# Reading the moving operand of the wide matmuls one column of each half in turn, in block attention followed by a feed-forward layer

## The chip, the cores and the metric

The kernel runs on one core of one Trainium2 chip. The metric is the device time of one execution in microseconds, lower is better; the figure of a kernel is the median of its runs.

## The reference

```python
scores = scale * np.matmul(q_c, k_c.transpose(0, 1, 2, 4, 3))   # chunks of 64 tokens, float32
attn = np.exp(scores - np.max(scores, axis=-1, keepdims=True))
attn = attn / (np.sum(attn, axis=-1, keepdims=True) + 1e-09)
out = np.matmul(attn, v_c)                                       # (8, 8, 576, 64)
x = out.transpose(0, 2, 1, 3).reshape(4608, 512)
h = x @ w_in                                                     # w_in (512, 2048), float64
g = h * np.cos(h)
return (g @ w_out).astype(np.float32)                            # w_out (2048, 512), float64
```

Attention works inside chunks of 64 tokens. Nearly all of the arithmetic is in the two products with `w_in` and `w_out`.

## The kernel before

The 4608 tokens are cut into 9 tiles of 512 (`TOK`). `w_in` and `w_out` are cut into 16 blocks each (`fc`, 128 of the 2048 inner features). A number that goes into a wide product is split into a high and a low part, both in the 4-byte type fp32r, and a product is made of three matmuls: high by high, high by low, low by high, all adding to the same bank of sums. So every product has three matmuls, each with a stationary operand of 128x128 (its weight load is an instruction of its own, PEld) and a moving operand of 128 partitions by 512 columns, or 256 in a few places.

- The hidden layer: `hidden` (line 859) for tiles 0 and 1, and `product` (line 1107) for the others, take a block of `w_in` (or sums and differences of blocks, "combos", kept in HBM and streamed back) as the stationary operand and the transposed tokens `x` as the moving one. The sums are `h` (in banks named h and a): 128 inner features on the partitions, 512 tokens as columns. Tile 2 (`FAST`) is paired with itself: two halves of 256 tokens, so its matmuls have 256 columns (`single_pair`). Tiles 3 to 8 go in pairs (`wide_pair`, `second_tile`), with 512 columns.
- `g = h cos h` is made by ScalarE and VectorE, split into `g_hi` and `g_lo` (lines 500 and 504; the low parts go to VectorE or GpSimd).
- The output layer: `projected_by_parts` (line 895) for tiles 0 and 1, and `out_part` (line 1160) for the others, take 128 columns of `g` (a quarter `sub` of the tile's tokens) as the stationary operand and a block of `w_out`, 512 columns, as the moving one. The sums are `acc`, one bank for each of four quarters: 128 tokens on the partitions, 512 output features as columns. They run over the blocks `fc`.
- `finish` (line 920) copies a bank of finished sums to SBUF (line 500 on ScalarE, line 498 on VectorE; for tile 0, whose first 8 blocks were stored apart as `partial`, line 939 adds) and stores 128 rows of the output (line 942), one DMA for each quarter. The last quarter of the last tile is made and stored in two halves of 256 output features.

All matmuls are issued by the one helper at line 494, so a row of the trace is told apart by its tiles: `h<-x,w_in`, `h<-w_in,w_in` and `a<-x,w_in` are hidden layer, `acc<-w_out,...` are output layer, `kt,qt` and `pts,vt` are attention. All DMAs are issued on SP's queue.

The order of the work is made when the program is built: each piece of work has an engine, a length, what it waits for, and a due time from long lists (`DUE_FIRST` and so on), and a planner (`placed`, `in_order`) lays them out; instructions then keep that order on each engine. The planner counts 0.68 us for three matmuls of 512 columns, 0.706 for six of 256 and 1.362 for six of 512.

```python
        matmul(o, g_hi[:, ss], w_hi[:, cols], start=first, stop=False, **on)
        matmul(o, g_hi[:, ss], w_lo[:, cols], start=False, stop=False, **on)
        matmul(o, g_lo[:, ss], w_hi[:, cols], start=False, stop=last, **on)
```

In `split_weight` (line 564, issued from the pieces it returns) ScalarE reads every second 4-byte word of the float64 weights, a read with a step of 8 bytes.

Of the kernel before, what the change touches and what calls it, by code (L numbers as in the profile page):

```python
# [21 lines left out]
P = 128  # L22
TOK = 512
# [12 lines left out]
FAST = 2  # L36
# [53 lines left out]
PE, ACT, DVE, POOL, SP = range(5)  # L90
# [369 lines left out]
def attention_then_cos_ffn(ctx: ExitStack, tc, qT, kT, v, w_in, w_out, out, wide):  # L460
# [4 lines left out]
    nc = tc.nc  # L465
    NT, HP = qT.shape[0], qT.shape[1]
    NFC, NCC = w_in.shape[1], w_in.shape[2]
    DM = out.shape[1]
    NCH = TOK // CH
    NSUB = TOK // P  # L470
# [15 lines left out]
    def kept(ins):  # L486
        tc.keep_in_program_order(ins)
        return ins
# [4 lines left out]
    def matmul(*args, **kw):  # L493
        kept(nc.tensor.matmul(*args, **kw))  # L494

    def copy_by(by, out, in_):
        if by == DVE:
            kept(nc.vector.tensor_copy(out, in_))
        else:
            kept(nc.scalar.copy(out=out, in_=in_))  # L500
# [13 lines left out]
    w_parts = {}  # L514
# [71 lines left out]
    x_parts = {}  # L586
# [9 lines left out]
    def x_room(t, dtype):  # L596

        kind = (t + (t > 1)) % 2
        asked_x[kind] += 1
        return x_named(f"x{kind}_{asked_x[kind] % 4}", dtype)  # L600
# [30 lines left out]
    def bank(kind, i):  # L631
        if kind == "a":
            b = ps_a.tile([P, 512], F32, name=f"a{i % 2}")
        else:
            b = ps_o.tile([P, 512], F32, name=f"acc{i}")
        return b
# [218 lines left out]
    acc = {}  # L855

    partial = [hbm.tile([P, DM], F32, name=f"partial{sub}") for sub in range(NSUB)]

    def hidden(t, fc, ccs=range(4), h=None):
        if h is None:  # L860
            h = ps_h.tile([P, TOK], F32, name="h")
        w_hi, w_lo = w_parts["in", fc]
        for cc in ccs:
            x_hi, x_lo = (x[:, cc % 2] for x in x_parts[t, cc // 2])
            ws = slice(cc * P, (cc + 1) * P)
            matmul(h, w_hi[:, ws], x_hi, start=(cc == 0), stop=False)
            matmul(h, w_hi[:, ws], x_lo, start=False, stop=False)
            matmul(h, w_lo[:, ws], x_hi, start=False, stop=(cc == NCC - 1))
        return h
# [25 lines left out]
    def projected_by_parts(s, sums_out):  # L895

        t, fc = order[s]
        first = s == 0 or order[s - 1][0] != t
        last = s == len(order) - 1 or order[s + 1][0] != t

        def part(sub):
            g_hi, g_lo = g_parts[t, fc]
            w_hi, w_lo = w_parts["out", fc]
            if first:
                acc[sub] = bank("acc", sub)
            o = acc[sub]
            ss = slice(sub * P, (sub + 1) * P)
            matmul(o, g_hi[:, ss], w_hi, start=first, stop=False)
            matmul(o, g_hi[:, ss], w_lo, start=False, stop=False)
            matmul(o, g_lo[:, ss], w_hi, start=False, stop=last)  # L910
            if last:
                sums_out.append(lambda by=None, sub=sub, o=o: finish(t, sub, o, fc == NFC - 1, by))

        return [lambda sub=sub: part(sub) for sub in range(NSUB)]

    def out_room(sub):

        return (wts if sub % 2 else dec).tile([P, DM], F32, name=f"half{sub // 2}" if sub % 2 else "w")

    def finish(t, sub, o, whole, by, cols=None):  # L920
        r0 = t * TOK + sub * P
        to = out[r0 : r0 + P, :]
        if t == 1 or not whole:

            os = att.tile([P, DM], F32, name="vt" if sub % 2 else "pts")
            to = to if whole else partial[sub]
        elif t == 0:
            os = acc["partial", sub]
        elif t < NT - 1:
            os = out_room(sub)  # L930
        else:

            if ("x", sub // 2) not in acc:
                acc["x", sub // 2] = x_room(t + 1, F32)
            os = acc["x", sub // 2][:, sub % 2]
            if cols:
                to, os, o = to[:, cols], os[:, cols], o[:, cols]
        if whole and t == 0:
            kept(nc.vector.tensor_tensor(os, os, o, op=ALU.add))
        else:  # L940
            copy_by(by or (ACT if t == NT - 1 and sub % 2 else DVE), os, o)
        nc.sync.dma_start(out=to, in_=os)

    def resume():

# [161 lines left out]
    def product(n, out, x_hi, x_lo, begin=False):  # L1107
        w, fc = streamed[n // 2]
        w = w[:, n % 2]
        for cc in range(2):  # L1110
            w_hi, w_lo = w[:, 0, cc], w[:, 1, cc]
            matmul(out, w_hi, x_hi[:, cc], start=begin and cc == 0, stop=False, skip_group_check=True)
            matmul(out, w_hi, x_lo[:, cc], start=False, stop=False, skip_group_check=True)
            matmul(out, w_lo, x_hi[:, cc], start=False, stop=cc == 1, skip_group_check=True)
        if n % 2 and fc in KEPT_ROOMS:
            load_two(fc)

# [36 lines left out]
    def first_fc(t):  # L1154
        return 1 if t == FAST else 0

    def last_fc(t):
        return NFC - 2 if t == FAST else NFC - 1

    def out_part(t, fc, sub, cols=slice(None)):  # L1160
        g_hi, g_lo = g_parts[t, fc]
        w_hi, w_lo = w_parts["out", fc]
        first, last = fc == first_fc(t), fc == last_fc(t)
        if first:
            acc[sub] = bank("acc", sub)
        o = acc[sub][:, cols]
        ss = slice(sub * P, (sub + 1) * P)
        on = dict(skip_group_check=True) if cols.start else {}
        matmul(o, g_hi[:, ss], w_hi[:, cols], start=first, stop=False, **on)
        matmul(o, g_hi[:, ss], w_lo[:, cols], start=False, stop=False, **on)  # L1170
        matmul(o, g_lo[:, ss], w_hi[:, cols], start=False, stop=last, **on)

    work = []

    def piece(eng, length, run, *after, at=0.0, lag=0.15, port=False, table=None, other=None, pairs=0, main=False):


        if eng != PE:
            length *= SAFE
        other = other and (other[0], SAFE * other[1], lag, other[2])  # L1180
        work.append([eng, length, run, [a for a in after if a is not None], at, length + lag, port, table, other, pairs, main])
        return len(work) - 1
# [11 lines left out]
    for what in FIRST_LOADS + [(name, fc) for fc in range(NFC) for name in ("in", "out")]:  # L1194
        if what not in here:
            mb, begin = begin_load.get(what[0], (0.5, load_weight))
# [10 lines left out]
    def rest_of(key, i):  # L1207
        return lambda *by: made[key][i](*by)
# [5 lines left out]
    for fc in range(NFC):  # L1214
        s = fc if fc < GROUP else GROUP + fc
# [4 lines left out]
    for i, (name, fc) in enumerate(turn_of):  # L1220
# [6 lines left out]
        h = piece(ACT, 0.52, rest_of(key, 3), joined[name, fc], other=(DVE, 0.45, True))  # L1227
# [77 lines left out]
    first = early(0)  # L1305
# [66 lines left out]
    for s in range(STAGE):  # L1372
        t, fc = order[s]
# [52 lines left out]
        a = piece(ACT, 0.53, begin_g, hid, given.get(s - 2), lag=0.2)  # L1426
        for i, (eng, length) in enumerate(((DVE, 0.6), (ACT, 0.55), (DVE, 0.6), (ACT, 0.53), (DVE, 0.6)), 1):
            a = piece(
                eng, length, rest_of(key, i), a, *([projected.get(s - LAG)] if i == 4 else ()),
                port=i == 5, table=AF.Sin if i == 2 else None, other={4: (DVE, 0.45, True), 5: (POOL, 1.25, False)}.get(i),  # L1430
            )
# [17 lines left out]
    for k in range(IN_LIST):  # L1449
        used = hids[GROUP + 2 * k + 1 + (NFC - GROUP if 2 * k >= GROUP else 0)]  # L1450
        a = piece(
            DVE, 1.38, lambda by, k=k: whole_again(k, by), used, lows[-1], *split.values(),
            port=True, other=(POOL, 2.5, False),
        )
        a = piece(DVE, 1.7, lambda by, k=k: sums_of_w(k, by), a, port=True, other=(POOL, 3.6, False))
# [3 lines left out]
        a = piece(ACT, 1.5, lambda k=k: high_parts(k), a, kept_blocks[k])  # L1459
# [14 lines left out]
    a = None  # L1474
    for j in (S1, S3, S2, A22):
        a = whole_x[j] = piece(DVE, 0.69, of_x(0, j), a, *ready, port=True)
    parts_x = []
    for j in (A11, S3, S2, A12, A22, S1, S4):
        a = piece(ACT, 0.55, of_x(1, j), whole_x.get(j, whole_x[S1]), other=(DVE, 0.45, True))
# [17 lines left out]
    low_of = {}  # L1497
    acc_free = {}
# [41 lines left out]
        return readers.get(name, ())  # L1540

    def out_piece(t, fc, sub, half=None):
        cols = slice(None) if half is None else slice(half * DM // 2, (half + 1) * DM // 2)
        p = pe(
            0.68 if half is None else 0.35, lambda: out_part(t, fc, sub, cols), low_of.get((t, fc)), acc_free.get(sub) if fc == first_fc(t) else None
        )
        spent.setdefault((t, fc), []).append(p)
        if fc == last_fc(t):
            if t == 0:
                acc_free[sub] = piece(DVE, 0.7, lambda: finish(t, sub, acc[sub], True, None), p)  # L1550
            elif half is not None:
                piece(ACT, 0.4, lambda: finish(t, sub, acc[sub], True, ACT, cols), p)
            else:
                acc_free[sub] = piece(
                    ACT, 0.62, lambda by: finish(t, sub, acc[sub], True, by), p, other=(DVE, 0.69, False)
                )
# [454 lines left out]
    for u in range(1, UNITS):  # L2011
        t = FAST + 2 * u + 1
# [87 lines left out]
```

## Time and profile before

| | |
|---|---|
| median of 3 runs | 818.65 us (817.99 to 819.93) |
| span of the profiled execution | 816.4 us, 2.25 us under that median |
| PE busy | 805.6 us (99%) |
| DVE, ACT, POOL busy | 582.8, 467.6, 306.1 us |
| 512-column matmuls | 3114 |
| mean DMA rate | 191 GB/s |

Times are in microseconds unless marked ns. PE is TensorE's matmuls, PEld its weight loads, DVE VectorE, ACT ScalarE, POOL GpSimd, SP SyncE, and SPq is SP issuing. The median stands for the whole device time; the span is counted from the first to the last instruction of the one execution that was profiled. A matmul's duration in a row overlaps with its neighbours', so the pace of a stream is read from the starts.

### The profile page before, as it was taken

The numbers are of one execution on the slowest core, as the hardware profiler recorded it, in microseconds if no ns is written. First come the engines' busy times: TensorE is split into PE (matmuls) and PEld (weight loads), VectorE is DVE, ScalarE is ACT, GpSimd is POOL, SyncE is SP. The second block draws the span as 40 slices with busy tenths as digits, with TensorE's granted clock in tenths as the row PEclk, the third lists the DMA queues.
The fourth block names the chain that finished last, engine by engine and source line by source line (L and its number), as shares of the span: only waits on it lengthen the run. The fifth ranks groups of instructions, "written<-read, shape, count | busy, mean of one in ns | idle before, by whom it ended". The sixth has DMA issues, their size and how long they took to land.

```text
span 816.4 us, 15169 instructions
## 1 busy us (share of the span) xinstructions
PE 805.6 (99%) x5818; PEld 670.8 (82%) x5818; DVE 582.8 (71%) x913; ACT 467.6 (57%) x872; POOL 306.1 (37%) x240
## 2 busy tenths in 40 slices
PE   7999999999999999999999999999999999999998
PEld 5888888888889888888888888888888888888887
DVE  6999988887887897875885957876787564553521
ACT  6998855465866567545654456544653464554522
POOL 3455565557634382201233922121265521121100
PEclk9999999999999999999999999999999999999999
DMA  9991624475876667546555367456553265543431
GB/s 344 411 416 68 233 100 175 165 274 192 300 245 202 203 212 249 180 150 231 175 162 174 104 213 267 165 168 221 159 202 83 74 215 161 177 167 106 154 91 65
DMA packets 71896, 156.18 MB, mean 191 GB/s; under 512 B 7184, under 2 KB 21776, under 8 KB 71824
## 3 DMA queue, kind: packets, MB, share of 16 engines
q1 hardware_dynamic: 71824, 155.22, 55.5%
q8 instruction: 46, 0.75, 0.4%
q14 instruction: 26, 0.21, 0.1%
HBM read 117.44 MB, written 37.75 MB: 190 GB/s over the span
## 4 chain that ended last, share of the span: by engine, by line
PE 96%; DVE 1%; ACT 1%; DMA 0%; issue 0%; SPq 0%; ACTq 0%
PE acc L494 49%; PE h L494 38%; PE a L494 10%; DMA kt<-in_kT_dram 0%; ACT e L673 0%; ACT e L716 0%; DVE z L753 0%; DVE m L661 0%; PE a L772 0%; DVE w L559 0%; DVE x L846 0%; DVE e L665 0%; ACT L673 0%; ACT L1132 0%; ACT e L737 0%
## 5 line engine op out<-in xcount | busy, mean ns | idle before, releaser
L494 PE MATMUL acc<-w_out,g_hi 128*128 128x512 f32 x1124 | 347.4, 390 | 0.0
L494 PEld LDWEIGHTS acc<-w_out,g_hi 128*128 128x128 f32 x1124 | 208.1, 188 | 42.2
L504 POOL TENSOR_TENSOR g_lo<-g,g_hi 128x512 fp32r<-128x512 f32 x78 | 111.4, 1430 | 300.0 <-ACT g_hi L500 196.4
L494 PE MATMUL acc<-w_out,g_lo 128*128 128x512 f32 x562 | 218.5, 389 | 0.0
L494 PE MATMUL h<-x,w_in 128*128 128x512 f32 (+1 forms) x864 | 207.1, 366 | 0.3 <-DVE g L1135 0.3
L494 PEld LDWEIGHTS h<-x,w_in 128*128 128x128 f32 x864 | 150.3, 188 | 28.7 <-DVE g L1135 0.7
L494 PE MATMUL h<-w_in,w_in 128*128 128x512 f32 (+1 forms) x576 | 141.4, 363 | 0.5 <-DVE w_in L1122 0.5
L494 PEld LDWEIGHTS acc<-w_out,g_lo 128*128 128x128 f32 x562 | 105.5, 188 | 22.3
L494 PEld LDWEIGHTS h<-w_in,w_in 128*128 128x128 f32 x576 | 99.3, 188 | 19.1 <-DVE w_in L1122 1.6
L500 ACT CAST g_hi<-g 128x512 fp32r<-128x512 f32 x98 | 60.5, 620 | 48.0 <-PE acc L494 35.4
L1128 DVE SCALAR_TENSOR_TENSOR g<-g,h 128x512 f32<-128x512 int32 (+1 forms) x40 | 23.1, 577 | 84.1 <-ACT g L1125 84.0
L494 PE MATMUL a<-x,w_in 128*128 128x512 f32 x288 | 73.2, 389 | 0.0
L494 PEld LDWEIGHTS a<-x,w_in 128*128 128x128 f32 x288 | 54.0, 188 | 11.4
L504 DVE TENSOR_TENSOR g_lo<-g,g_hi 128x512 fp32r<-128x512 f32 x38 | 35.5, 938 | 28.3 <-ACT g_hi L500 27.5
L1119 ACT COPY h<-h 128x512 f32<-128x512 f32 (+1 forms) x40 | 19.4, 485 | 60.8 <-PE h L494 54.7
L1132 ACT ACTIVATE g<-g 128x512 f32<-128x512 f32 (+1 forms) x72 | 42.0, 584 | 17.0 <-DVE g L1128 16.9
L881 ACT ACTIVATE g<-h 128x512 int32<-128x512 f32 x32 | 19.1, 596 | 30.5 <-PE h L494 25.9
L1132 ACT ACTIVATE w_in<-w_in 128x512 f32<-128x512 f32 x48 | 29.9, 629 | 10.7 <-DVE w_in L1128 10.6
L504 POOL TENSOR_TENSOR e<-e,z 128x512 f32<-128x512 f32 x14 | 17.9, 1291 | 43.6 <-DVE z L758 34.9
L500 ACT CAST g_hi<-w_in 128x512 fp32r<-128x512 f32 x24 | 15.0, 624 | 33.7 <-PE acc L494 33.7
L1125 ACT ACTIVATE g<-h 128x512 int32<-128x512 f32 (+1 forms) x40 | 20.5, 513 | 20.7 <-PE h L494 20.4
L882 DVE SCALAR_TENSOR_TENSOR g<-g,h 128x512 f32<-128x512 int32 x32 | 21.8, 682 | 14.3 <-ACT g L881 14.0
(205 smaller groups left out, 1182.1 us busy)
## 6 DMA issues: line engine op xcount, KB each, us to landing
w_in<-combo SPq DMA_DIRECT2D x112, 512.0 KB, 3.8
combo<-w_in SPq DMA_DIRECT2D x56, 256.0 KB, 3.3
gathered<-w_in SPq DMA_DIRECT2D x48, 256.0 KB, 2.5
qt<-in_qT_dram SPq DMA_DIRECT2D x36, 256.0 KB, 4.8
kt<-in_kT_dram SPq DMA_DIRECT2D x36, 256.0 KB, 5.2
w_in<-in_w_in_dram SPq DMA_DIRECT2D x16, 512.0 KB, 9.3
w_out<-in_w_out_dram SPq DMA_DIRECT2D x16, 512.0 KB, 9.6
w_in<-gathered SPq DMA_DIRECT2D x24, 256.0 KB, 2.9
```

The costliest lines, as they stand in the source:

```text
L494: kept(nc.tensor.matmul(*args, **kw))
L500: kept(nc.scalar.copy(out=out, in_=in_))
L504: kept(eng.tensor_tensor(out, a, b, op=op))
L881: lambda: kept(nc.scalar.activation(n, h, AF.Identity, bias=0.25, scale=0.5 / math.pi)),
L882: lambda: kept(nc.vector.scalar_tensor_tensor(g, n, -2.0 * math.pi, h, op0=turns, op1=over)),
L1119: kept(nc.scalar.copy(out=out, in_=in_))
L1125: kept(nc.scalar.activation(g.bitcast(I32), h, AF.Identity, bias=0.25, scale=0.5 / math.pi))
L1128: kept(nc.vector.scalar_tensor_tensor(g, g.bitcast(I32), -2.0 * math.pi, h, op0=ALU.mult, op1=ALU.add))
L1132: kept(nc.scalar.activation(g, g, AF.Sin, bias=0.5 * math.pi))
```

## The change

Every wide matmul reads its moving operand through a view that takes column 0 of the first half, column 0 of the second half, column 1 of the first half, and so on. The sums of the hidden layer, and with them `g`, then hold the tokens in that order, and the sums of the output layer hold the output features in that order. The copy out of the bank puts the features back (it reads every second sum), and the store puts the tokens back: each quarter is stored by two DMAs, of the even and of the odd partitions, 64 rows each. Weights, the number of matmuls, the banks and the planner's lengths stay.

```diff
+    def crossed(a, first=0, n=None):
+        a = a.rearrange("p (n k) -> p k n", n=2)
+        return a[:, first : first + n] if n else a
...
     def hidden(...)
-            x_hi, x_lo = (x[:, cc % 2] for x in x_parts[t, cc // 2])
+            x_hi, x_lo = (crossed(x[:, cc % 2]) for x in x_parts[t, cc // 2])
...
     def projected_by_parts(...)
-            w_hi, w_lo = w_parts["out", fc]
+            w_hi, w_lo = (crossed(w) for w in w_parts["out", fc])
...
+    def rows_of(t, sub):
+        rows = out[t * TOK : (t + 1) * TOK, :]
+        if t == FAST:
+            return rows.rearrange("(h b s a) d -> h s a b d", h=2, b=2, s=NSUB // 2)[sub // 2, sub % 2]
+        return rows.rearrange("(b s a) d -> s a b d", b=2, s=NSUB)[sub]
+
-    def finish(t, sub, o, whole, by, cols=None):
-        r0 = t * TOK + sub * P
-        to = out[r0 : r0 + P, :]
+    def finish(t, sub, o, whole, by, half=None):
...
-            if cols:
-                to, os, o = to[:, cols], os[:, cols], o[:, cols]
+        flat, os, o = os, os.rearrange("p (n k) -> p n k", n=2), o.rearrange("p (k n) -> p n k", n=2)
+        some = slice(None) if half is None else slice(half * DM // 4, (half + 1) * DM // 4)
+        os, o = os[:, :, some], o[:, :, some]
...
-        nc.sync.dma_start(out=to, in_=os)
+        if not whole:
+            nc.sync.dma_start(out=partial[sub], in_=flat)
+            return
+        for b in range(2):
+            to = rows_of(t, sub)[:, b].rearrange("a (n k) -> a n k", n=2)[:, :, some]
+            nc.sync.dma_start(out=to, in_=os[b::2])
...
     def product(...)
-            matmul(out, w_hi, x_hi[:, cc], start=begin and cc == 0, stop=False, skip_group_check=True)
-            matmul(out, w_hi, x_lo[:, cc], start=False, stop=False, skip_group_check=True)
-            matmul(out, w_lo, x_hi[:, cc], start=False, stop=cc == 1, skip_group_check=True)
+            hi, lo = crossed(x_hi[:, cc]), crossed(x_lo[:, cc])
+            matmul(out, w_hi, hi, start=begin and cc == 0, stop=False, skip_group_check=True)
+            matmul(out, w_hi, lo, start=False, stop=False, skip_group_check=True)
+            matmul(out, w_lo, hi, start=False, stop=cc == 1, skip_group_check=True)
...
-    def out_part(t, fc, sub, cols=slice(None)):
+    def out_part(t, fc, sub, half=None):
         g_hi, g_lo = g_parts[t, fc]
-        w_hi, w_lo = w_parts["out", fc]
+        some = () if half is None else (half * DM // 4, DM // 4)
+        cols = slice(None) if half is None else slice(half * DM // 2, (half + 1) * DM // 2)
+        w_hi, w_lo = (crossed(w, *some) for w in w_parts["out", fc])
...
-        matmul(o, g_hi[:, ss], w_hi[:, cols], start=first, stop=False, **on)
+        matmul(o, g_hi[:, ss], w_hi, start=first, stop=False, **on)
```

The attention part is not touched.

## Rows read from the trace of the kernel before

**Rows 1.** The list of cores: span, and mean granted clock as a share of full speed.

```profile
core 0: 816.4 us, clock 1.000
```

**Rows 2.** The page: busy time, share of the span and instructions of each engine; and the chain that ended last, as shares of the span by engine and by line.

```profile
PE 805.6 (99%) x5818; PEld 670.8 (82%) x5818; DVE 582.8 (71%) x913; ACT 467.6 (57%) x872; POOL 306.1 (37%) x240
...
PE 96%; DVE 1%; ACT 1%; DMA 0%; issue 0%; SPq 0%; ACTq 0%
PE acc L494 49%; PE h L494 38%; PE a L494 10%; DMA kt<-in_kT_dram 0%; ACT e L673 0%; ACT e L716 0%; DVE z L753 0%; DVE m L661 0%; PE a L772 0%; DVE w L559 0%; DVE x L846 0%; DVE e L665 0%; ACT L673 0%; ACT L1132 0%; ACT e L737 0%
```

**Rows 3.** The waits of PE, longest first: who waited for whom, us in total, times, the longest.

```profile
PE acc L494 <- DMA kt<-in_kT_dram: 1.8, 3, 1.0
PE h L772 <- POOL e L504: 1.5, 3, 0.8
PE a L1302 <- POOL ident masks.py:199: 1.4, 1, 1.4
```

**Rows 4.** Groups of PE's instructions, shapes kept apart: count, then busy us and mean ns of one, then idle time before.

```profile
L494 PE MATMUL acc<-w_out,g_hi 128*128 128x512 f32 x1116 | 345.9, 391 | 0.0
L494 PE MATMUL acc<-w_out,g_lo 128*128 128x512 f32 x558 | 217.4, 390 | 0.0
L494 PE MATMUL h<-x,w_in 128*128 128x512 f32 x672 | 181.7, 390 | 0.0
L494 PE MATMUL h<-w_in,w_in 128*128 128x512 f32 x432 | 121.5, 390 | 0.0
L494 PE MATMUL a<-x,w_in 128*128 128x512 f32 x288 | 73.2, 389 | 0.0
L494 PE MATMUL h<-x,w_in 128*128 128x256 f32 x192 | 25.5, 281 | 0.3 <-DVE g L1135 0.3
L494 PE MATMUL h<-w_in,w_in 128*128 128x256 f32 x144 | 19.9, 282 | 0.5 <-DVE w_in L1122 0.5
...
L494 PE MATMUL acc<-w_out,w_in 128*128 128x512 f32 x48 | 12.4, 394 | 0.0
...
L494 PE MATMUL acc<-w_out,g_hi 128*128 128x256 f32 x8 | 1.5, 282 | 0.0
...
L494 PE MATMUL acc<-w_out,g_lo 128*128 128x256 f32 x4 | 1.1, 282 | 0.0
```

**Rows 5.** The chain that ended last, in order of time: start us, us, what. The `h ... x24` pieces are matmuls of 256 columns, the `acc` ones of 512 (the last also holds 12 of 256).

```profile
243.09 2.87 PE h L494 x24
...
262.10 2.84 PE h L494 x24
...
423.48 21.76 PE acc L494 x96
...
595.95 21.76 PE acc L494 x96
...
761.41 51.78 PE acc L494 x234
...
813.21 0.37 ACT x L500
```

**Rows 6.** Busy time of each engine in three stretches in which the chain is output layer alone: the stretch and its length, then PE, PEld, DVE, ACT, POOL, the granted clock, the busy share of the DMA engines and GB/s.

```profile
423.48:445.24 21.76, 21.76 (x101) 17.74 (x102) 14.67 (x26) 10.39 (x19) 9.74 (x7) 1.00 0.61 196
595.95:617.71 21.76, 21.76 (x101) 17.74 (x101) 14.33 (x24) 9.98 (x18) 11.12 (x9) 1.00 0.61 197
761.41:808.62 47.21, 47.21 (x210) 39.06 (x209) 12.71 (x19) 13.44 (x23) 1.29 (x1) 1.00 0.35 112
```

**Rows 7.** Single output-layer matmuls in order of time, near the end: start us, us, what. Two matmuls of high parts start between one of these and the next.

```profile
807.26 0.39 PE L494 MATMUL acc<-w_out,g_lo 128*128 128x512 f32 x1
...
808.62 0.39 PE L494 MATMUL acc<-w_out,g_lo 128*128 128x512 f32 x1
```

**Rows 8.** The page's group of weight loads for the output layer.

```profile
L494 PEld LDWEIGHTS acc<-w_out,g_hi 128*128 128x128 f32 x1124 | 208.1, 188 | 42.2
```

**Rows 9.** Groups of ScalarE: a straight read of SBUF (line 500, a cast), the read of every second word (line 564), and copies out of a bank of sums, whole and half.

```profile
L500 ACT CAST g_hi<-g 128x512 fp32r<-128x512 f32 x98 | 60.5, 620 | 48.0 <-PE acc L494 35.4 <-DVE g L884 5.2 <-DVE g L1135 4.1
...
L564 ACT ACTIVATE w<-w_in 128x512 f32<-128x512 f32 x16 | 10.7, 678 | 1.1 <-DVE w_out L504 0.5 <-POOL w_in L504 0.3 <-DVE w_in L504 0.3
...
L500 ACT COPY half<-acc 128x512 f32<-128x512 f32 x12 | 7.1, 589 | 2.5 <-PE acc L494 2.0
...
L500 ACT COPY x<-acc 128x256 f32<-128x256 f32 x2 | 0.7, 373 | 0.2
```

**Rows 10.** Busy time of each engine in the first stages, columns as in rows 6.

```profile
0.00:20.00 20.00, 14.40 (x292) 12.21 (x292) 11.93 (x22) 11.98 (x35) 6.44 (x11) 1.00 0.92 343
20.00:60.00 40.00, 39.49 (x360) 32.38 (x349) 37.48 (x64) 38.57 (x65) 20.39 (x16) 1.00 1.03 414
60.00:129.00 69.00, 69.00 (x423) 56.85 (x422) 61.22 (x84) 51.46 (x93) 40.30 (x31) 1.00 0.40 142
```

**Rows 11.** The same stretch for the matmuls of line 494 alone: PE and PEld.

```profile
20.00:60.00 40.00, 38.24 (x344) 30.57 (x333) 1.00 1.03 414
```

**Rows 12.** The stores of line 942 on SP's queue: duration of one issue in ns, least, median and most; first and last start.

```profile
L942 SPq DMA_DIRECT2D out_dram<-w x12: 332/338/382, 313.1 to 768.9; - x12
L942 SPq DMA_DIRECT2D out_dram<-x x9: 332/332/338, 218.8 to 813.6; - x9
```

**Rows 13.** The end in order of time: start us, us, what.

```profile
809.66 4.29 SPq L942 DMA_DIRECT2D out_dram<-x  x5
```

More of the change, by code (lines that the diff above doesn't have):

```diff
@@ L918, in out_room @@
         return (wts if sub % 2 else dec).tile([P, DM], F32, name=f"half{sub // 2}" if sub % 2 else "w")
-    def finish(t, sub, o, whole, by, cols=None):
-        r0 = t * TOK + sub * P
-        to = out[r0 : r0 + P, :]
+    def rows_of(t, sub):
[4 more added lines that the diff above has]
+    def finish(t, sub, o, whole, by, half=None):
         if t == 1 or not whole:
             os = att.tile([P, DM], F32, name="vt" if sub % 2 else "pts")
-            to = to if whole else partial[sub]
         elif t == 0:
@@ L1168, in out_part @@
         on = dict(skip_group_check=True) if cols.start else {}
-        matmul(o, g_hi[:, ss], w_hi[:, cols], start=first, stop=False, **on)
-        matmul(o, g_hi[:, ss], w_lo[:, cols], start=False, stop=False, **on)
-        matmul(o, g_lo[:, ss], w_hi[:, cols], start=False, stop=last, **on)
+        matmul(o, g_hi[:, ss], w_hi, start=first, stop=False, **on)
+        matmul(o, g_hi[:, ss], w_lo, start=False, stop=False, **on)
+        matmul(o, g_lo[:, ss], w_hi, start=False, stop=last, **on)
     work = []
@@ L1542, in out_piece @@
     def out_piece(t, fc, sub, half=None):
-        cols = slice(None) if half is None else slice(half * DM // 2, (half + 1) * DM // 2)
         p = pe(
-            0.68 if half is None else 0.35, lambda: out_part(t, fc, sub, cols), low_of.get((t, fc)), acc_free.get(sub) if fc == first_fc(t) else None
+            0.68 if half is None else 0.35, lambda: out_part(t, fc, sub, half), low_of.get((t, fc)),
+            acc_free.get(sub) if fc == first_fc(t) else None,
         )
@@ L1551, in out_piece @@
             elif half is not None:
-                piece(ACT, 0.4, lambda: finish(t, sub, acc[sub], True, ACT, cols), p)
+                piece(ACT, 0.4, lambda: finish(t, sub, acc[sub], True, ACT, half), p)
             else:
```

## The prediction

> **What bounds the kernel now.** I read the span first: one core, 816.4 us, granted clock 1.000, so TensorE runs at the upper of its two levels (2.4 GHz) all through [rows 1]. Then the busy line and the chain that ended last: PE is busy 99% of the span, and 96% of the chain is PE, in three groups of tiles, all of line 494 [rows 2]. PE's own waits, the third view, add up to a few microseconds, nearly all of them for the first loads [rows 3]. So no engine stands in front of PE; what counts is how fast it gets through its matmuls.
>
> The groups by form give the work [rows 4]. The 512-column matmuls are 1116 + 558 + 672 + 432 + 288 + 48 = 3114, the 256-column ones 192 + 144 + 8 + 4 = 348. Their means (390 and 281 ns) are durations of overlapping instructions; the pace has to be read from starts. The chain in order of time gives it: 96 matmuls of 512 columns take 21.76 us, twice, which is 226.7 ns each [rows 5]. At 2.4 GHz 512 columns are 213.3 ns. So each takes 544 cycles where 512 would do: 17 cycles for every 16 columns, 13.3 ns too many, and 3114 x 13.3 = 41 us of the span in all. The 256-column ones go 24 in 2.84 to 2.87 us, some 118 ns, where 256 cycles are 106.7 [rows 5].
>
> What are these 32 cycles? Not the neighbours: two stretches with DVE busy for 14.67 of 21.76 us and DMA at 0.61 keep the same 226.7 ns as the last stretch, with DVE at 12.71 of 47.21 and DMA at 0.35 [rows 6], where six matmuls start in 1.36 us [rows 7]. Not the weight loads: one takes 188 ns, under 226.7, and lies beside the matmul before it [rows 8]. What is left is the stream itself: the moving operand's read, or the write of the sums. That the excess is 17/16 speaks for something that comes every 16 columns; in this operand, 4 bytes a column in one straight run, that is every 64 bytes of a partition. No row shows which of the two it is.
>
> **The change, part by part.**
>
> *The order of the read.* Nothing is removed or added on PE: the same matmuls, weights and banks, and the planner's lengths (0.68 for three, 0.706, 1.362) are not touched, so its order of work stays. Each 512-column read jumps 1024 bytes at every column, to the other half and back. If the lost cycle belongs to the step from one 64-byte piece to the next in a straight run, two runs read in turn can make the step of one while the other delivers. No row has such a read, so I bound it on both sides. Best: all 32 cycles go, 13.3 ns. Less, if part of the excess is a fixed cost: a straight line through 226.7 (512) and 118 (256) has 0.4246 ns a column, 0.0079 over 1/2.4, so the order could give back 512 x 0.0079 = 4.1 ns only. Worst: a read that pays for each jump. The nearest row is ScalarE's read with a step of 8 bytes, 678 ns against 620 for a straight one [rows 9], 1.094 times as long: 248 ns, 21 more. At the far end every column takes two cycles: 426.7 ns, 200 more. I take 11 ns gained, so 215.7 ns. It is nearest to the all-goes end since 544 is exactly 17/16 in each long stretch, and since the 256-column pieces vary (2.84 and 2.87 us), which says that something else holds those. For them I take no gain; at most 348 x 11.3 = 3.9 us.
>
> 3114 x 11 = 34.3 us. Less what PE can't use: up to 60 us the DMA engines are loaded through (0.92 and 1.03) and DVE is busy for 37.48 of 40 us [rows 10]; line 494 is busy for 38.24 us between 20 and 60 us [rows 11], at most 169 wide matmuls, 1.9 us; I take 1.5, as small ones share that time. Later DVE's fullest stage, 60 to 129 us, goes from 61.22 of 69.00 to 61.22 of some 65.6, 93%: still below, but with small new waits, for which I take 1.5 us. Gain on PE: 31.3 us.
>
> *The copies out of the accumulators.* 36 blocks, and 4 partial ones, read every second sum. They cost 589 ns on ScalarE, the halves 373 [rows 9]. By the 8-byte row up to 9.4% more, 55 ns; by nothing less than zero. All but the last lie beside PE: a bank is free again long before PE comes back to it, since three other banks of three matmuls each (2 us) stand between, and PE shows no wait for such a copy [rows 3]. If that cover were gone, 40 x 0.055 = 2.2 us. The last one, 373 ns, is on the path: 0.03 us.
>
> *The stores.* Each of 37 stores of whole rows becomes two, of every second partition. SP spends 332 to 338 ns on each issue [rows 12], so 37 x 0.335 = 12.4 us more on a queue that nowhere sets PE's pace; loads queued behind a block's second store go 0.34 us later, up to 1.3 us after the four blocks of a tile, and the streamed weights behind them are asked for a room or more ahead. At the end nothing hides them: the chain ends in the last copy [rows 5], the last store is issued when that copy is done, and the five stores of the end take 4.29 us from first to last [rows 13]. There the block before puts its second issue (to about 0.2 us after the last copy) and the last half adds its own (0.335): 0.5 us later, between 0.3 and 0.9, since its pieces shrink from 1 KB to 512 bytes.
>
> **Sum**: 818.65 - 31.3 + 0.5 = 788 us. The profiled execution has a span of 816.4, 2.25 us under the median of the three runs; the terms are differences, so they hold against either, and I set them against the median.
>
> **Rivals.**
>
> *Half pace (slower).* Place: the moving read of each wide matmul. If the reader holds one short line of memory and fetches again for every column that lies elsewhere, the turn order makes it fetch 512 times instead of once for several columns. It decides from the point where a fetch costs more than the 32 cycles saved, one cycle in 16 columns. Price, by two cycles a column: 3114 x 200 + 348 x (213.3 - 118) = 623 + 33 us, so 1475 us; by ScalarE's ratio, 3114 x 21 = 65 us, so 884. For it: that the only stepped read with a straight one beside it is slower [rows 9]. Against: that step was small and the engine another, at another width; and the order comes back to the same place every second column, so that a reader that holds two lines pays nothing. [...]
>
> *Nothing (no change).* The excess isn't the read's: the write of sums, or a pause that the array makes whatever feeds it. PE keeps 226.7 ns; only the tail is left, 818.65 + 0.5 = 819.2. For it: the trace can't part read from write. Against: nothing.
>
> *Another bound.* The stream gets its 215.7 ns, but the finely ordered queues of DVE, ScalarE and SP, laid out for 226.7, come late, and half the gain turns into waits: 818.65 - 17 = 802 us. DVE in the stage of 60 to 129 us would be first [rows 10]. Against: over the whole span DVE has 582.8 us of work and ScalarE 467.6 [rows 2], far under 785.
>
> **How the numbers follow.** Forecast (the stream faster, most of it kept): 0.61. Another bound: 0.08. Nothing: 0.10. Slower: 0.21, of which some 0.14 at half pace. A measurement of this kernel tells some 0.2% from no change, 1.6 us. Faster 0.69, same 0.10, slower 0.21. The likeliest is 788. The range: down to the best end, 3114 x 13.3 + 3.9 = 45 us less, of which some 2 stay behind, 775; up over "another bound" and "nothing" with a longer tail, 822. That leaves out the slower cases, 0.21. The forecast's own range is 775 to 806 (4.1 ns gained would be 818.65 - 12.8 + 0.5 = 806).
>
> **What would show it.** In the profile after: 96 such matmuls of the chain in 20.7 us (21.76 if nothing; 23.8 or 41 if slower); PE still 99% busy; PE's waits still a few microseconds (if 15 or more, another bound); copies out of acc up to 640 ns; twice as many stores on SP at some 335 ns each, with nobody waiting for them but the end; the time between the last matmul and the end 0.5 us longer. What would make it wrong: a 512-column matmul every 227 ns or more.

## The result and the profile after

| | before | after |
|---|---|---|
| median | 818.57 us (4 runs) | 792.96 us (4 runs, 792.41 to 793.24) |
| ratio | | 0.9686, 95% interval 0.9672 to 0.9700 |
| span of the profiled execution | 816.4 us | 790.4 us |
| from the last matmul of the chain to the end of the span | 816.4 - 813.19 = 3.2 us | 790.4 - 785.07 = 5.3 us |

The change gains 25.6 us; 788 us (30.6 less than before) had been forecast. The first view to read again is the chain in order of time: the same pieces as in [rows 5].

```profile
22.80 7.25 DMA w_in<-in_w_in_dram
...
250.84 2.72 PE h L494 x24
...
256.82 1.34 PE h L494 x12
...
258.81 2.79 PE h L494 x24
...
413.52 20.72 PE acc L494 x96
...
578.18 20.72 PE acc L494 x96
...
735.80 49.27 PE acc L494 x234
785.07 0.02 issue
785.09 0.37 ACT x L505
```

96 output-layer matmuls take 20.72 us, 215.8 ns each (518 cycles), where [rows 5] had 21.76 and 226.7 (544). Cycles are counted at 2.4 to the ns, an estimate: where the granted clock is 0.50 (below), matmuls of 512 columns start 427 ns apart, so at one column a cycle they would take 213.5 ns at the full clock. A piece of 24 matmuls of 256 columns takes 2.72 or 2.79 us against 2.84 and 2.87, and one of 12 takes 1.34 us (111.7 ns each). In the kernel before, such a piece of 12 took 1.41 (117.5):

```profile
260.00 1.41 PE h L494 x12
```

At those paces the long matmuls give back 3114 x 10.9 = 33.9 us, and the 348 short ones, at some 6 ns each, about 2.1 us: 36 us. The span fell by 26.0. The other 10 us are in the rest of the profile.

The windows, columns as in [rows 6], show three places; the second line is line 494 alone, as in [rows 11]:

```profile
20.00:60.00 40.00, 38.86 (x348) 32.40 (x349) 35.80 (x63) 39.58 (x62) 19.75 (x15) 1.00 1.03 414
...
174.00:190.00 16.00, 14.21 (x67) 12.12 (x66) 10.88 (x16) 8.92 (x18) 12.17 (x12) 1.00 0.78 274
...
226.00:240.00 14.00, 12.00 (x176) 10.36 (x175) 9.88 (x22) 7.75 (x21) 4.39 (x4) 0.88 0.66 214
```

```profile
20.00:60.00 40.00, 36.82 (x332) 30.63 (x333) 1.00 1.03 414
```

From 20 to 60 us PE gets through no more matmuls of line 494 than before (332 against 344 in [rows 11]), each shorter, in the same 40 us with DMA at 1.03: PE waits there for its weights, and the chain has their loads (the line at 22.80 us). From 174 to 190 us PE is busy for 14.21 of 16. From 226 to 240 us it is busy for 12.00 of 14, and the granted clock is 0.88. VectorE's timeline and PE's waits name the last two:

```profile
176.69 0.69 DVE L1094 TENSOR_TENSOR vt<-e,e 128x512 f32<-128x512 f32 x1 [2.04 <-DMA out_dram<-vt]
...
182.84 0.87 DVE L1094 TENSOR_TENSOR pts<-e,pts 128x512 f32<-128x512 f32 x1 [3.05 <-DMA out_dram<-pts]
```

```profile
PE h L494 <- DVE g L889: 2.4, 3, 1.8
PE a L494 <- issue: 2.0, 1, 2.0
```

At 176 and 182 us VectorE makes differences for tile 2's hidden layer in rooms (`vt`, `pts`) from which tile 1's output is still being stored. It waits 2.0 and 3.1 us for those stores; the multiplication for g (line 889) stands behind it on the same queue, and PE waits for that (1.8 us at 184.9 us). In the kernel before, VectorE waited 0.9 us for the store of `vt` and not at all for that of `pts`, and PE did not wait there.

The wait of 2.0 us for "issue" stands in the middle of the attention matmuls of 64 columns, at 231.4 us, with nothing that this view shows to wait for. It is not new: before the same matmul PE pauses for 0.64 us in the kernel before. After the 2.0 us the granted clock is 0.50 for 3.4 us (233.4 to 236.8 us), and matmuls of 512 columns start 427 ns apart (three in 1.28 us):

```profile
233.84 1.22 PE L494 MATMUL acc<-w_out,g_hi 128*128 128x512 f32 x2
234.85 0.63 PE L494 MATMUL acc<-w_out,g_lo 128*128 128x512 f32 x1
235.28 1.06 PE L494 MATMUL acc<-w_out,g_hi 128*128 128x512 f32 x2
236.13 0.63 PE L494 MATMUL acc<-w_out,g_lo 128*128 128x512 f32 x1
```

The stores, answering to [rows 12] and [rows 13], and the copies, answering to [rows 9]:

```profile
L958 SPq DMA_DIRECT2D out_dram<-w x24: 472/544/597, 308.3 to 744.2; - x24
...
L958 SPq DMA_DIRECT2D out_dram<-x x18: 471/580/604, 214.5 to 787.5; - x18
```

```profile
781.77 6.31 SPq L958 DMA_DIRECT2D out_dram<-x  x10
```

```profile
L505 ACT COPY half<-acc 128x512 f32<-128x512 f32 x12 | 7.1, 590 | 2.0 <-PE acc L494 1.5 <-DMA out_dram<-half 0.2
...
L505 ACT COPY x<-acc 128x256 f32<-128x256 f32 x2 | 0.7, 372 | 0.2
```

Issuing a store of 64 rows takes SP 544 to 580 ns, where one of 128 rows took 332 to 338. So a quarter costs SP about 1.1 us instead of 0.34, and the end, where four issues stand behind the last copy, is 2.1 us longer. The copies with a step of 8 bytes cost what they did: 590 and 372 ns against 589 and 373.

### The profile page after: what moved, and what is told of

Same layout as the page of the kernel before. It is cut to its first block, busy times and chain, and to the rows that moved or that the text cites. A ratio compares the mean times of both kernels' runs of the same rounds, so it can differ in the third digit from the quotient of the medians.

```text
span 790.4 us, 15213 instructions
## 1 busy us (share of the span) xinstructions
PE 772.8 (98%) x5818; PEld 673.7 (85%) x5818; DVE 579.6 (73%) x913; ACT 473.4 (60%) x872; POOL 302.8 (38%) x240
## 4 chain that ended last, share of the span: by engine, by line
PE 85%; ACT 6%; DMA 4%; DVE 3%; issue 1%; POOL 0%; SPq 0%; ACTq 0%; DVEq 0%; POOLq 0%
PE acc L494 44%; PE h L494 32%; PE a L494 9%; DMA w_in<-in_w_in_dram 2%; DMA qt<-in_qT_dram 1%; ACT half L571 1%; ACT w L569 1%; ACT g L888 0%; ACT g L886 0%; DMA out_dram<-pts 0%; ACT g_hi L505 0%; PE a L1321 0%; ACT e L678 0%; DVE pts L509 0%; DMA out_dram<-vt 0%
## 5 line engine op out<-in xcount | busy, mean ns | idle before, releaser
L494 PE MATMUL acc<-w_out,g_hi 128*128 128x512 f32 x1124 | 336.3, 381 | 0.6 <-ACT pts L505 0.6
L509 POOL TENSOR_TENSOR g_lo<-g,g_hi 128x512 fp32r<-128x512 f32 x78 | 109.8, 1410 | 282.7 <-ACT g_hi L505 178.0
L494 PE MATMUL acc<-w_out,g_lo 128*128 128x512 f32 x562 | 213.1, 379 | 0.0
L494 PE MATMUL h<-x,w_in 128*128 128x512 f32 (+1 forms) x864 | 199.0, 357 | 2.9 <-DVE g L889 2.4
L494 PE MATMUL h<-w_in,w_in 128*128 128x512 f32 (+1 forms) x576 | 136.2, 354 | 0.8 <-DVE w_in L1139 0.7
L494 PE MATMUL a<-x,w_in 128*128 128x512 f32 x288 | 70.2, 380 | 0.0
L1145 DVE SCALAR_TENSOR_TENSOR w_in<-w_in,w_in 128x512 f32<-128x512 int32 x24 | 28.6, 1190 | 2.4 <-ACT w_in L1142 1.2
L888 ACT ACTIVATE g<-g 128x512 f32<-128x512 f32 x32 | 20.2, 631 | 14.6 <-DVE g L887 14.5
```

Source lines behind the costliest of these rows:

```text
L509: kept(eng.tensor_tensor(out, a, b, op=op))
L888: lambda: kept(nc.scalar.activation(g, g, AF.Sin, bias=0.5 * math.pi)),
L1145: kept(nc.vector.scalar_tensor_tensor(g, g.bitcast(I32), -2.0 * math.pi, h, op0=ALU.mult, op1=ALU.add))
```

## The experiments

Theory at the start (theory 1, the prediction's): a straight run loses a cycle at each step to the next 64 bytes, and a second run in turn hides it. Rival: neighbours cost (theory 2). The first four kernels take the change apart.

**Output layer alone.**

```diff
-            x_hi, x_lo = (crossed(x[:, cc % 2]) for x in x_parts[t, cc // 2])
+            x_hi, x_lo = (x[:, cc % 2] for x in x_parts[t, cc // 2])
...
-            hi, lo = crossed(x_hi[:, cc]), crossed(x_lo[:, cc])
+            hi, lo = x_hi[:, cc], x_lo[:, cc]
...
-        for b in range(2):
-            ...
+        to = rows_of(t, sub).rearrange("a (n k) -> a n k", n=2)[:, :, some]   # rows in order
+        nc.sync.dma_start(out=to, in_=os)
...
```

> Only the output layer reads its moving operand (w_out) in the turned order; the tokens stay straight, so each quarter is one store again. Theory (the order of the read sets the pace of the matmul that has it, and of no other): 96 output-layer matmuls in 20.72 us, the hidden layer's 512-column ones at 226.7 ns and its 256-column ones at 118; 1722 x 10.9 ns = 18.8 us gained, about 1 of it lost while the first loads arrive, and the end after the last matmul back at 3.2 us: 801 us. Rival (the gain comes from something the two layers share, such as the banks or the weight loads between them): the hidden layer's pace changes too, or the output layer's is not 20.72; the time is not near half of the way.

803.71 us (803.44 to 804.46); ratio 0.9812 (0.9797 to 0.9826) to a median of 819.32 on the same chip. In the chain, a stretch that has both layers:

```profile
320.84 2.59 PE acc L494 x12
323.43 1.38 PE h L494 x6
...
330.14 2.74 PE h L494 x12
```

The turned matmuls go 12 in 2.59 us (215.8 ns), the straight ones beside them 12 in 2.74 (228.3; in the kernel before 2.72): the pace belongs to the matmul that has the order. The straight ones lose 1.7 ns against the kernel before, which over 1392 is 2.3 of the 2.7 us by which the time is above the 801 expected; why they lose it was not tested. The rival, something that both layers share, falls.

**Hidden layer alone.**

```diff
-            w_hi, w_lo = (crossed(w) for w in w_parts["out", fc])
+            w_hi, w_lo = w_parts["out", fc]
...
-        w_hi, w_lo = (crossed(w, *some) for w in w_parts["out", fc])
+        w_hi, w_lo = (w[:, cols] for w in w_parts["out", fc])
...
-        flat, os, o = os, os.rearrange("p (n k) -> p n k", n=2), o.rearrange("p (k n) -> p n k", n=2)
+        flat = os
...
```

> Only the hidden layer reads its moving operand (x) in the turned order; the tokens are then in that order, so each quarter keeps two stores. Theory: 96 output-layer matmuls in 21.76 us, the hidden layer's 512-column ones at 215.8 ns, 24 of its 256-column ones in 2.7 us: 1392 x 10.9 + 348 x 6 ns = 17.3 us gained; the two stores cost 2.1 us at the end and about 2 before: 805 us. Rival (two stores cost nothing but the half microsecond of the prediction): 802 us.

810.81 us (809.83 to 813.26); ratio 0.9901 (0.9883 to 0.9920). The paces are those of the theory, the time is 6 us above it and 9 above its rival:

```profile
328.14 2.73 PE acc L494 x12
...
333.46 2.59 PE h L494 x12
```

```profile
PE a L494 <- issue: 1.9, 1, 1.9
...
PE h L494 <- DVE g L889: 1.2, 1, 1.2
```

The end takes 807.9 - 802.88 = 5.0 us, and PE waits 1.2 us behind line 889, as in the changed kernel; the 4 us allowed for the stores cover that. The pause among the attention matmuls is 1.9 us here, with 3.4 us at the lower clock after it: some 2.8 us more. So the 6 us can't all be put down to the stores. The two halves together gain 15.6 + 8.5 = 24.1 us, the whole change 25.6.

**The two stores alone.** The change with both edits above to the matmuls, the stores left as two.

> The kernel before with the two stores a quarter alone: all matmuls straight, each quarter stored as the even and the odd partitions to 64 rows each (so the rows of the output stand in another order). Theory (the stores cost about 2.1 us at the end and up to 2 us in waits behind SP's queue): 821 to 823 us, issues of some 560 ns. Rival (they cost only where PE is faster, or the 0.5 us of the prediction): 819 us.

824.00 us (823.36 to 824.48); ratio 1.0057 (1.0040 to 1.0073): this kernel is 4.7 us slower than the one before, with no matmul changed, and above both expectations. VectorE's waits for the stores are there as in the changed kernel, the one for `pts` longer, PE waits 2.1 us behind line 889, and the end takes 822.1 - 817.00 = 5.1 us, 1.9 more than before:

```profile
181.79 0.69 DVE L1094 TENSOR_TENSOR vt<-e,e 128x512 f32<-128x512 f32 x1 [1.74 <-DMA out_dram<-vt]
...
188.91 1.19 DVE L1094 TENSOR_TENSOR pts<-e,pts 128x512 f32<-128x512 f32 x1 [4.02 <-DMA out_dram<-pts]
```

```profile
PE h L494 <- DVE g L889: 2.1, 1, 2.1
```

```profile
817.00 0.02 issue
817.03 0.37 ACT x L505
```

These two make 4.0 us. Some 0.6 us of the rest was lost before 20 us, ahead of any such store, so the stores' own cost is nearer 4 than 4.7.

**One store a quarter.** The tokens are put back where the output layer loads its weights: every second column of g.

```diff
+    def quarter(g, t, sub):
+        if t == FAST:
+            return g.rearrange("p (h k n) -> p h n k", h=2, n=2)[:, sub // 2, sub % 2]
+        return g.rearrange("p (k n) -> p n k", n=2)[:, sub // 2, sub % 2 * P : (sub % 2 + 1) * P]
...
-            matmul(o, g_hi[:, ss], w_hi, start=first, stop=False)
+            hi, lo = quarter(g_hi, t, sub), quarter(g_lo, t, sub)
+            matmul(o, hi, w_hi, start=first, stop=False)
...
-        for b in range(2):
-            ...
+        to = rows_of(t, sub).rearrange("a (n k) -> a n k", n=2)[:, :, some]   # rows in order
+        nc.sync.dma_start(out=to, in_=os)
...
```

> All wide matmuls in the turned order as in the change, but the tokens are put back where the output layer loads its weights (every second column of g, a step of 8 bytes), so that a bank holds 128 tokens in a row and each quarter is one store of 128 rows. Theory (the second store and the longer issues of 64 rows cost some 4 us in waits and at the end; a stepped weight load stays hidden beside the matmul): SP's issues back at some 335 ns, the end after the last matmul back at 3.2 us, 96 matmuls still in 20.72 us: 789 us. Rival (the stepped weight load is slower, by up to 1.09 as ScalarE's read is, or by two, 380 ns): at 207 ns it is still hidden, 789; at 380 ns the output layer is paced by it, 96 matmuls in 36 us, and the kernel is far slower than before, some 1070 us.

787.06 us (786.61 to 787.16); ratio 0.9606 (0.9592 to 0.9620), below the change's whole interval: some 6 us better, and the best of all kernels run.

```profile
L494 PEld LDWEIGHTS acc<-w_out,g_hi 128*128 128x128 f32 x1124 | 217.5, 196 | 22.9 <-ACT pts L510 1.0
```

```profile
409.91 20.72 PE acc L494 x96
...
732.12 49.36 PE acc L494 x234
781.48 0.02 issue
```

```profile
L960 SPq DMA_DIRECT2D out_dram<-w x12: 332/338/382, 304.7 to 739.3; - x12
```

The stepped weight load takes 196 ns instead of 188 [rows 8] and stays under 215.8; the pace is kept; SP's issues are back at 338 ns and the end at 784.9 - 781.48 = 3.4 us. The granted clock is 1.000 over the whole span. Set beside the changed kernel matmul by matmul (PE's order is the same), the one-store kernel gains 1.9 us at the end, 2.0 us between 170 and 226 us, where PE no longer waits behind line 889, and 2.4 us between 226 and 300 us, where the pause among the attention matmuls is shorter and the clock does not fall; it loses 0.7 us before 84 us.

**Other orders of the columns**, in the changed kernel with only `crossed` changed; one execution each. One `+` line stands for one kernel. The sums are written in the same order in all of them.

```diff
-        a = a.rearrange("p (n k) -> p k n", n=2)
...
+        return a.rearrange("p (k n) -> p n k", n=2)              # even, then odd
+        return a.rearrange("p (n m k) -> p m n k", n=2, k=2)     # two by two
+        return a.rearrange("p (n m k) -> p m n k", n=2, k=16)    # sixteen by sixteen
+        return a.rearrange("p (m n k) -> p m k n", n=2, k=16)    # near
+        return a.rearrange("p (n k) -> p k n", n=4)              # quarters
+        return a.rearrange("p (n m e) -> p e m n", n=2, e=2)     # turned, step 8
+        return a.rearrange("p (n m e) -> p e m n", n=2, e=4)     # turned, step 16
```

> The changed kernel with another order of the columns: all even ones, then all odd ones, a step of 8 bytes (the output's columns and rows then stand in another order, here and in the next three). Theory 1 (a straight run loses one cycle at every step to the next 64 bytes, and a second run in turn hides it): 64 such steps, 576 cycles, 96 matmuls in 23.0 us. Theory 2 (it is two columns side by side, one right after the other, that cost the cycle now and then, so any order that never reads neighbours is free): 20.7 us. [...]

1556.44 us:

```profile
785.33 43.31 PE acc L494 x96
```

> The changed kernel with two neighbouring columns of each half in turn. Theory 1 (two runs hide each other's steps): 96 matmuls in 20.72 us. Theory 2 (neighbours cost): half of the successions are neighbours, half of the 32 cycles, 21.2 us. [...]

1149.99 us:

```profile
584.91 31.49 PE acc L494 x96
```

> The changed kernel with sixteen neighbouring columns (64 bytes) of each half in turn. Theory 1, where the next piece of the same run is got ready while the other half delivers: 96 matmuls in 20.72 us; theory 1, where what costs is that the reader leaves a piece at all: 21.76 us. Theory 2 (neighbours cost): 15 of 16 successions are neighbours, 21.7 us.

863.14 us:

```profile
444.73 23.04 PE acc L494 x96
```

> The changed kernel with one column in turn from two neighbouring pieces of 64 bytes (a jump of 64 bytes instead of 1024). Theory 1, wherever the two runs lie: 96 matmuls in 20.72 us. If the two runs have to lie in different parts of the memory, far apart: 21.76 us or more. Theory 2 (neighbours cost): 20.72 us.

788.62 us:

```profile
409.75 20.72 PE acc L494 x96
```

Theories 1 and 2 both fall with the first of these: neighbours are never read in a row, and it takes 451 ns a matmul, twice the straight read (226.7). A price on each jump as such falls with the change itself, where every column lies some 1024 bytes from the one before it: 215.8 ns. What these times suggest is that the pace goes with the step from a column to the next but one: 4 bytes in the change and in "near" (20.72 us), 8 in the straight read (21.76), 16 in "even, then odd" (43.31). The next three orders were made to test that. Expected by it were 31 us or more for the quarters, where this step goes 1024 bytes on and back as in "two by two" (31.49), 21.76 us for the halves in turn in steps of 8 bytes, and 43.3 us for those in steps of 16.

> The changed kernel with one column of each of four quarters in turn (the output's columns and rows stand in another order, here and in the next two). Theory 1 (several runs in turn hide each other's steps to the next 64 bytes): 96 matmuls in 20.72 us. [...]

1000.66 us:

```profile
510.43 27.20 PE acc L494 x96
```

> The changed kernel with the halves in turn, but in each half first the even columns and then the odd ones, so each half is read in steps of 8 bytes. [...] Theory 1 (two runs in turn): 20.72 us. Theory 2 (neighbours cost): 20.72 us.

825.22 us:

```profile
428.30 21.76 PE acc L494 x96
```

> The same with every fourth column of each half, steps of 16 bytes. [...] Theories 1 and 2: 20.72 us.

1556.68 us:

```profile
785.68 43.31 PE acc L494 x96
```

The table sorts the nine orders by the step from a column to the next but one:

| order | bytes from a column to the next but one | us for 96 | cycles a matmul |
|---|---|---|---|
| halves in turn (the change); near | 4 | 20.72 | 518 |
| straight; turned, step 8 | 8 | 21.76 | 544 |
| sixteen by sixteen | 8, with a jump after 8 columns | 23.04 | 576 |
| even, then odd; turned, step 16 | 16 | 43.31 | 1083 |
| two by two | 1024, then 1016 back | 31.49 | 787 |
| quarters | 1024, then 1020 back | 27.20 | 680 |

In the first, second and fourth row this step is 4, 8 and 16 bytes, at even and at odd places alike, but for the jumps from one piece to another. Each of these rows has two orders, and the two take the same time to the hundredth of a microsecond; for "turned, step 8" and "turned, step 16" that had been expected beforehand, against theories 1 and 2. The expectation missed on quarters (27.20, not 31 or more), and sixteen by sixteen is 32 cycles slower than the row with 8 bytes: what a jump costs is not settled, and no run shows why the step to the next but one counts.

**The planner told the new pace**, on the kernel with one store.

```diff
-            0.68 if half is None else 0.35, lambda: out_part(t, fc, sub, half), ...
+            0.6475 if half is None else 0.335, lambda: out_part(t, fc, sub, half), ...
-                PE, 2.72, made_by(key, hidden, t, fc), ...
+                PE, 2.59, made_by(key, hidden, t, fc), ...
```

(and 0.706 to 0.67, 1.362 to 1.295.)

> The kernel with one store a quarter (tokens put back in the weight load), and the planner told the new pace: 0.6475 us for three matmuls instead of 0.68, 2.59 for twelve instead of 2.72, 0.67 and 1.295 for six; the due times stay. Theory (what is left of the gain, about 4 us, is lost to queues laid out for the old pace): 784 to 786 us. Rival (it is lost where the first loads set the pace and where PE waits for nothing that the profile shows; a new layout on due times made for the old one brings waits of its own): 787 to 792 us.

817.65 us (816.75 to 819.56, 10 runs); ratio 0.9983 (0.9973 to 0.9994). Both expectations fall: the new layout loses 30 us, nearly the whole gain, while the pace stays (96 in 20.72 us):

```profile
PE h L494 <- DVE g L1154: 4.8, 2, 3.6
PE h L494 <- DVE w_in L1141: 4.4, 3, 2.9
PE h L494 <- DVE g L894: 4.2, 4, 2.5
```

```profile
0.00:60.00 60.00, 50.86 (x623) 43.34 (x624) 47.78 (x82) 50.06 (x95) 23.78 (x24) 0.98 0.99 389
60.00:300.00 240.00, 225.92 (x1916) 200.34 (x1915) 199.54 (x342) 159.25 (x335) 107.25 (x100) 0.98 0.55 186
300.00:764.00 464.00, 455.18 (x3050) 403.60 (x3050) 325.91 (x487) 253.22 (x421) 148.85 (x100) 1.00 0.52 177
```

PE is idle for 9.1 us up to 60 us, 14.1 from there to 300 and 8.8 from there to 764, and in the first two stretches the mean granted clock is 0.98. The due times were chosen for the old lengths; with the lengths alone changed the order is a worse one. What a layout made anew would bring was not tried.

## Why the prediction came out as it did

*What bounds the kernel*: right. PE is still busy for 98%, and the time follows the pace of its matmuls. The clock's two levels stand in the trace of the changed kernel (1.00, and 0.50 for 3.4 us); the 2.4 GHz taken for the upper one is an estimate that fits the 427 ns at the lower, if a column takes one cycle.

*The size of the gain on the stream*: right, 10.9 ns a matmul where 11 was taken (20.72 us for 96, 20.7 forecast). *Its reason*: wrong. The step between 64-byte pieces would have made "even then odd" 23.0 us and "turned, step 8" 20.72; they took 43.31 and 21.76. The pace went instead with the step between one column and the next but one: 8 bytes in the straight read, 4 in the turned one, 16 in the slow orders (518, 544 and 1083 cycles for 4, 8 and 16). Why that step counts no run shows, and the orders that jump among those columns (576, 680 and 787 cycles) don't go by it alone. So the size was right in part by luck: the reason given for it is not the cause. The rival "nothing", with the write of the sums as the cause, falls, since all orders write the sums alike.

*The rival at half pace*: its price was real, its condition was not. The slowest orders take 1083 cycles (451 ns), a little over two a column, and the kernel 1556 us (1475 had been worked out). But the change is not such a read: it goes elsewhere at every column and takes 518 cycles, while "even, then odd", which goes on in steps of 8 bytes, takes 1083. So the measurement decides against a price for each column that lies elsewhere; what the reader holds of the memory no run shows, and the 0.14 for this rival was the author's estimate. ScalarE's 8-byte step [rows 9] said nothing on it: 678 ns against 620 there, 451 against 226.7 for TensorE in "even, then odd".

*The 256-column matmuls*: no gain was taken, for lack of an explanation of their 118 ns. They gained about 6 ns each, 2.1 us, half of what they took over 256 cycles (118 against 106.7 ns): the order of the read was part of their excess too.

*What PE can't use*: 3.0 us was taken. It was 36.0 - 2.1 - 26.0 = 7.9 us. Matmul by matmul against the kernel before, 2.1 us of it are missing by 84 us, where 3.0 had been foreseen by 129 us. The rest was not in VectorE's fullest stage but in two places: 2.0 us between 170 and 190 us, the wait behind the stores of tile 1, and 2.9 us between 226 and 245 us, the pause at 231 us and the slower clock after it. The doubled stores cause the first: VectorE's wait for `pts` (2.5 to 4.0 us), and PE's behind it (0.7 to 2.1 us), stand in all six kernels with two stores a quarter whose long matmuls take 240 ns or less, and in none of the three with one store and the same layout. The pause at 231 us does not go by the stores: the order "near" has the same stores and the same pace, and pauses for 1.2 us with no fall of the clock after it, as the kernel with one store does. At those paces the pause is in every kernel with this layout, 0.64 us in the one before and 1.0 to 2.0 us in the others, always at the same place in PE's order. It ends 2.3 to 2.6 us after a packet of 16 KB of the page's DMA kind "instruction" begins to move (in the change 230.87 and 233.42 us). Whether the two belong together no run tests, and the cause stays open.

*The copies*: the lower bound, nothing, was right (590 and 372 ns).

*The stores*: the step that failed. It took 335 ns for each issue, from rows of 128 partitions; with 64, every second partition, an issue takes 544 to 580. So SP had some 30 us more to do (43.2 us in 74 issues, against 13.6 in 37), not 12.4, the end cost 2.1 us instead of 0.5, and the rooms that the stores read were not free in time: the stores alone cost some 4 of the 4.7 us measured, and taking them back gained 6, of which 2.4 lie at the pause whose cause is open.

The forecast lies 5 us under the time: what PE can't use was 4.9 us more than taken and the end 1.6 us more, while the short matmuls gave 2.1 us that had not been counted.

## What to carry to other kernels

Here a stream of matmuls whose starts lay further apart than its columns over the clock (226.7 ns against some 213), by a constant ratio and in every stage alike, was paced by its own reads. Where a profile shows the same, try the order in which it reads, and test the reason with orders that separate the explanations, since the gain can be right for a wrong one. Put a changed order back where a slack engine or a hidden load can do it (here the weight load, 8 ns of cover used), rather than on SP's queue, where it cost some 30 us of issues, and waits behind them. A planner's lengths and its due times belong together: here correcting one without the other cost nearly the whole gain.

## What the runs showed that was not expected

- A fp32r matmul of 512 columns takes from 518 to 1083 cycles (215.8 to 451 ns) at the full clock by the order of its moving operand alone; straight (544) is not the fastest.
- The length of the jump did not matter in the turned read: two pieces 64 bytes apart and two halves 1024 bytes apart give the same 20.72 us. Jumps are not free in every order: sixteen by sixteen, two by two and quarters (23.04, 31.49 and 27.20 us) are all slower than the straight read (21.76).
- Splitting a store of 128 partitions into two of every second partition costs SP 1.1 us instead of 0.34.
- The granted clock fell to 0.50 after a pause of 2.0 us among small matmuls (231 to 233 us), and not in the kernel with one store, where that pause was 1.2 us. Nor did it fall in the changed kernel after the pause of 1.8 us at 184.9 us, among matmuls of 512 columns.
